# Block-sparse attention, then a gated MLP, on one core: gate and value products taken in turns, and more filler matmuls at the start

## The chip, the core and the metric

The kernel runs on one core of a Trainium2 chip. The metric is the device time of one execution in microseconds (us), the median over several runs. A core has a matrix engine (TensorE, PE in the profile; its weight loads are shown as PEld), VectorE (DVE), ScalarE (ACT), GpSimd (POOL), and SyncE (SP), which here only issues DMAs. Each engine takes its instructions in program order; they wait for one another through semaphores. [...]

## What is computed

The reference, cut to what matters (4 batches, 8 heads, 768 positions, head size 64, so a model width of 512; d_ff is 1024):

```python
scores = scale * np.matmul(q, k.transpose(0, 1, 3, 2))
scores = np.where(mask, scores, -1000000000.0)   # blocks of 32: band, first, last, sampled
attn = softmax(scores)
x = attn @ v                                      # heads side by side: (4, 768, 512)
...
h = np.maximum(x @ w_in, 0.0)
u, v = (h[..., :d_ff // 2].copy(), h[..., d_ff // 2:].copy())
mu = np.mean(v, axis=-1, keepdims=True)
var = np.mean((v - mu) ** 2, axis=-1, keepdims=True)
v_n = (v - mu) / np.sqrt(var + 1e-06)
v_s = np.einsum('ts,bsd->btd', w_spatial, v_n) + b_spatial[None, :, None]
gated = u * v_s
return (gated @ w_out).astype(np.float32)
```

The second part is the gMLP. Half of `x @ w_in` is the gate u, the other half is the value v. Every position's v is normalized over its 512 features; the spatial product then mixes all 768 positions, so it needs all of the normalized v of a batch.

## The kernel before, in words

**Attention.** The 32 heads are worked off one after another, two (a pair) per outer step `p`. A head's 768 keys are cut into six chunks of 128. One chunk of one head is a slot: two score matmuls of 384 columns (L289) into a PSUM tile with two buffers, one exp on ACT that empties it (L293), and, seven slots behind (`LAG`), the six matmuls of attention times values for one chunk of queries (L305). After the last chunk of a head DVE takes the reciprocal of the row sums and scales (L318, L319). The mask enters as 24 extra rows of q and k. The loads, the casts on POOL (L109, L112), the transposes (by PE in the first pairs, by DMA on SP's queue later) and DVE's copies into the head tiles (L244, L278) for the pairs to come are written into fixed slots of a pair.

**gMLP.** `moe_units` makes a list of single matmuls for one batch, in this order: value products (six chunks of 128 positions, four matmuls of 512 columns each), gate products (six of four), spatial products (six of six), output products (six of four): 108 matmuls. `add` (L376) makes the steps of one product: the first asks for a PSUM tile, the last calls the epilogue. The lists of batches 0, 1 and 2 go into a queue (`moe_q`, L524) once a batch's four pairs are through, and the loop hands out 108/48 = 2.25 matmuls per slot (108/52 for batch 2). These products share a PSUM tag, "moe", of two buffers: the third product from now cannot begin before the epilogue of the first has read its tile. Batch 3 is worked off after the attention (L529 to L532), with six buffers taken in rotation from three tags (`moe_ps(last)`).

**Epilogues.** A value product's `v_post` (L392) applies relu on DVE (L396; in the last batch on ACT, L394), then DVE's statistics (L399) and their aggregation into mean and variance (L400); after chunks 2 and 5, POOL adds epsilon (L403) and raises to the power -0.5 (L405), for three chunks at a time, into `rstd`. A gate product's `u_post` (L411) applies relu on ACT (L412), and DVE normalizes the value chunk of the same number (L413) into `vn`, which it can do once `rstd` is there. A spatial product reads the six chunks of `vn` in order, so its sixth matmul waits for the last of them; its epilogue multiplies by the gate (L430, DVE). In the last batch PE transposes the result (L423), in the others SP's queue does by DMA. An output product is copied out by ACT or DVE (L448, L450) and stored.

**Start.** While the first loads come in, PE runs filler matmuls on zeros (`keep_warm`, L178): eight of 512 columns, then small groups of 128 columns between the work that the first scores need. That work is, in PE's order: the transposes of k's first head (`tr_head`, L228, copied out by DVE, L220), two fillers, the mask product (L252, copied out by ACT), the transposes of q's first head (L228, copied by DVE), six fillers, then the first scores.

Of the kernel before, what the change touches and what calls it, by code (L numbers as in the profile page):

```python
# [10 lines left out]
FP32 = mybir.dt.float32  # L11
BF16 = mybir.dt.bfloat16
I32 = mybir.dt.int32
AF = mybir.ActivationFunctionType
ALU = mybir.AluOpType
# [11 lines left out]
def kernel(  # L27
# [16 lines left out]
    nc = tc.nc  # L44
# [5 lines left out]
    NCH = S // 128  # L50
    HALF = S // 2
    DM = H * D
    DFF = moe_w_in.shape[1]
    DH = DFF // 2
    NDM = DM // 128
# [8 lines left out]
    work = ctx.enter_context(tc.tile_pool(name="work", bufs=1))  # L64
# [5 lines left out]
    w_in_t = const.tile([128, NDM, DFF], BF16)  # L70
# [4 lines left out]
    mhalf = const.tile([128, NCH], FP32)  # L75
# [102 lines left out]
    def keep_warm(n, cols):  # L178
        for _ in range(n):
            nc.tensor.matmul(out=wps[:, 0:cols], lhsT=warm[:, 0:128], rhs=warm[:, 0:cols],  # L180
                             start=True, stop=True)
# [26 lines left out]
    for r in range(NR):  # L208
        nc.vector.scalar_tensor_tensor(out=allowed, in0=colidx,
                                       scalar=samp_f[:, 2 * r:2 * r + 1], in1=allowed,  # L210
                                       op0=ALU.is_equal, op1=ALU.max)
    bm = const.tile([NB, NB], BF16)
    nc.vector.tensor_scalar(out=bm, in0=allowed, scalar1=1.0, scalar2=-MASK_NEG,
                            op0=ALU.subtract, op1=ALU.mult)
# [3 lines left out]
                         func=AF.Copy)  # L218
# [3 lines left out]
    def act_copy(o, i):  # L222
        nc.scalar.activation(out=o, in_=i, func=AF.Copy)

    def tr_head(h, nm, copy):
        ps = psum.tile([128, S], BF16, tag="moe", bufs=2)
        for c in range(NCH):
            nc.tensor.transpose(out=ps[0:D, c * 128:(c + 1) * 128], in_=nat[nm, 0][:, c, h],  # L228
                                identity=ident)
        copy((qt if nm == "q" else kt)[h][0:D, :], ps[0:D, :])  # L230
# [15 lines left out]

    tr_head(0, "k", dve_copy)
    nc.vector.tensor_copy(out=kt[0][D:KR, :], in_=ind)
    keep_warm(2, 128)
    mq = psum.tile([128, 1024], FP32, tag="sc", bufs=2, name="mq")  # L250
    for hf in range(2):
        nc.tensor.matmul(out=mq[0:NB, hf * 512:hf * 512 + HALF], lhsT=bm,  # L252
                         rhs=ind[:, hf * HALF:(hf + 1) * HALF], start=True, stop=True)
    act_copy(qt[0][D:KR, :].rearrange("p (b c) -> p b c", b=2),
             mq[0:NB].rearrange("p (b c) -> p b c", b=2)[:, :, 0:HALF])
    tr_head(0, "q", dve_copy)
    keep_warm(6, 128)

    def mask_rows(sl):
        nc.vector.tensor_copy(out=kt[sl][D:KR, :], in_=kt[0][D:KR, :])  # L260
# [92 lines left out]
    def moe_ps(last):  # L353
        if not last:
            return psum.tile([128, 512], FP32, tag="moe", bufs=2, name="ps_moe")
        tail_tags.rotate(-1)
        if tail_tags[0] == "sc":
            return psum.tile([128, 1024], FP32, tag="sc", bufs=2, name="ps_sc")[:, 0:512]
        return psum.tile([128, 512], FP32, tag=tail_tags[0], bufs=2, name="ps_t")

    def moe_units(b):
        last = b == B - 1
        units = []
        un = work.tile([128, NCH, DH], BF16, tag="un", bufs=2)
        vsb = work.tile([128, NCH, DH], BF16, tag="vsb", bufs=2)
        vn = work.tile([128, NCH, DH], BF16, tag="vn", bufs=2)
        gn = work.tile([128, NCH, DH], BF16, tag="gn", bufs=2)
        gt = work.tile([128, NCH, NDH, 128], BF16, tag="gt", bufs=2)
        mv = work.tile([128, NCH, 2], FP32, tag="mv", bufs=2)
        std = work.tile([128, NCH], FP32, tag="std", bufs=2)  # L370
        rstd = work.tile([128, NCH], FP32, tag="rstd", bufs=2)

        def xt(g):
            return xt_ref[b * NG + g]

        def add(n, operands, post):  # L376


            box = []

            def step(i):
                if i == 0:
                    box.append(moe_ps(last))
                lhs, rhs = operands(i)
                nc.tensor.matmul(out=box[0], lhsT=lhs, rhs=rhs,  # L385
                                 start=(i == 0), stop=(i == n - 1))
                if i == n - 1:
                    post(box[0])
            units.extend((lambda i=i: step(i)) for i in range(n))

        for tcc in range(NCH):
            def v_post(ps, tcc=tcc):  # L392
                if last:
                    nc.scalar.activation(out=vsb[:, tcc, :], in_=ps, func=AF.Relu)  # L394
                else:
                    nc.vector.tensor_scalar(out=vsb[:, tcc, :], in0=ps, scalar1=0.0,  # L396
                                            scalar2=None, op0=ALU.max)
                stats = work.tile([128, 6], FP32, tag="stats", bufs=2)
                nc.vector.bn_stats(out=stats, in_=vsb[:, tcc, :])  # L399
                nc.vector.bn_aggr(out=mv[:, tcc, :], in_=stats)  # L400
                if tcc % 3 == 2:
                    cs = slice(tcc - 2, tcc + 1)
                    nc.gpsimd.tensor_scalar(out=std[:, cs], in0=mv[:, cs, 1], scalar1=1e-6,  # L403
                                            scalar2=None, op0=ALU.add)
                    nc.gpsimd.tensor_tensor(out=rstd[:, cs], in0=std[:, cs],  # L405
                                            in1=mhalf[:, cs], op=ALU.pow)
            add(NDM, lambda g, tcc=tcc: (xt(g)[:, tcc * 128:(tcc + 1) * 128],
                                         w_in_t[:, g, DH:DFF]), v_post)

        for tcc in range(NCH):  # L410
            def u_post(ps, tcc=tcc):  # L411
                nc.scalar.activation(out=un[:, tcc, :], in_=ps, func=AF.Relu)  # L412
                nc.vector.tensor_scalar(out=vn[:, tcc, :], in0=vsb[:, tcc, :],  # L413
                                        scalar1=mv[:, tcc, 0:1],
                                        scalar2=rstd[:, tcc:tcc + 1],
                                        op0=ALU.subtract, op1=ALU.mult)
            add(NDM, lambda g, tcc=tcc: (xt(g)[:, tcc * 128:(tcc + 1) * 128],
                                         w_in_t[:, g, 0:DH]), u_post)

        def g_tr(tcc):  # L420
            ps = psum.tile([128, S], BF16, tag="moe", bufs=2, name="ps_g")
            for dhc in range(NDH):
                nc.tensor.transpose(out=ps[:, dhc * 128:(dhc + 1) * 128],  # L423
                                    in_=gn[:, tcc, dhc * 128:(dhc + 1) * 128],
                                    identity=ident)
            act_copy(gt[:, tcc].rearrange("p c n -> p (c n)"), ps[:, 0:DH])

        for tcc in range(NCH):
            def s_post(ps, tcc=tcc):
                nc.vector.scalar_tensor_tensor(out=gn[:, tcc, :], in0=ps,  # L430
                                               scalar=b_col[:, tcc:tcc + 1],
                                               in1=un[:, tcc, :], op0=ALU.add, op1=ALU.mult)
                if not last:
                    nc.sync.dma_start_transpose(out=gt[:, tcc], in_=gn[:, tcc, :])
                elif tcc > 0:
                    g_tr(tcc - 1)
            add(NCH, lambda sc, tcc=tcc: (w_spt[:, sc, tcc * 128:(tcc + 1) * 128],
                                          vn[:, sc, :]), s_post)

        for tcc in range(NCH):  # L440
            def o_post(ps, tcc=tcc):
                osb = work.tile([128, DM], FP32, tag="osb", bufs=6)
                if last and tcc == NCH - 1:
                    nc.scalar.activation(out=osb[:, 0:DM // 2], in_=ps[:, 0:DM // 2],
                                         func=AF.Copy)
                    nc.vector.tensor_copy(out=osb[:, DM // 2:DM], in_=ps[:, DM // 2:DM])
                elif tcc % 2 == 0:
                    nc.scalar.activation(out=osb, in_=ps, func=AF.Copy)  # L448
                else:
                    nc.vector.tensor_copy(out=osb, in_=ps)  # L450
                nc.sync.dma_start(
                    out=out[b].rearrange("(p c) d -> c p d", c=NCH)[tcc], in_=osb)
            if last and tcc == 1:
                units.append(lambda: g_tr(NCH - 1))
            add(NDH, lambda dhc, tcc=tcc: (gt[:, tcc, dhc, :], w_out_t[:, dhc, :]), o_post)
        return units
# [7 lines left out]
    for p in range(NP + 1):  # L464
        for s in range(12):
            g = 12 * p + s
# [54 lines left out]
            if s == 8 and p >= NG:  # L521
                xtr(p - 1)
                if p % NG == 0:
                    moe_q.extend(moe_units(p // NG - 1))  # L524
                    slots_left = 48 if p < NP - NG else 52
                    budget = 0.0
    for _ in range(len(moe_q) // 2):
        moe_q.popleft()()
    xtr(NP - 1)  # L529
    moe_q.extend(moe_units(B - 1))  # L530
    while moe_q:
        moe_q.popleft()()  # L532
# [28 lines left out]
```

The softmax here doesn't subtract the row's maximum and nothing guards it: scores larger than these inputs give would overflow.

## Time and profile before

| | |
|---|---|
| median of 5 runs | 225.96 us (224.1 to 226.25) |
| the profiled execution, device time | 226.05 us |
| its span, first to last instruction | 224.3 us |
| first scores (L289) start | 8.04 us |
| first gMLP product starts | 50.7 us |
| first product of the last batch starts | 195.6 us |
| busy: PE, ACT, DVE, POOL | 216.6, 177.7, 128.7, 64.7 us |

The device time is 1.75 us longer than the span; all positions in the text are us from the span's start. In a line of the timeline or of a group, the tile written stands to the left of the arrow, the tiles read to the right; what stands in brackets is how long the engine sat idle before it and what released it. PE's instructions overlap, so that the duration of one is not its price: in a dense row a matmul of 512 columns starts 0.216 us after the one before it, though each is shown 0.38 long. The same holds for ACT: an exp is shown 0.82 long, and in a dense row six take 4.21 us.

### The profile page before, as it was taken

To read this page: it belongs to the slowest core of one execution; us is meant where nothing else is said; L and a number is where in the kernel's file an instruction comes from. 1 tells how busy PE (TensorE), PEld (TensorE's weight loads), DVE (VectorE), ACT (ScalarE), POOL (GpSimd) and SP (SyncE) were. 2 spreads that over 40 slices of the span, in tenths; PEclk is the share of its full clock that TensorE was granted. 3 is DMA by queue.
4 is the path that set the end of the run, shared out by engine and by line. 5 is a ranking of instruction groups with operands and counts; after the bars stand their busy time and mean duration, and the time that the engine had idled before them with its cause. 6 is when DMAs were issued, how large, how long until landed. Compare 5 with 4: busy or idle time off the path is not lost.

```text
span 224.3 us, 5316 instructions
## 1 busy us (share of the span) xinstructions
PE 216.6 (97%) x2148; PEld 130.6 (58%) x2148; DVE 128.7 (57%) x282; ACT 177.7 (79%) x246; POOL 64.7 (29%) x88
## 2 busy tenths in 40 slices
PE   7999999999999999999899999999999999999993
PEld 3567777775555655665556566566556655544551
DVE  5465554556984545268983454359993433584531
ACT  5599999998789888887699888888899885266351
POOL 5435751429950801210650301210620000012000
PEclk9999999999999999999999999999999999999999
DMA  6689989895799676999756296999050224620015
GB/s 200 222 294 390 382 287 378 286 127 61 219 296 149 229 119 158 232 293 279 238 105 214 47 109 190 223 291 271 3 105 5 57 50 82 212 96 0 0 52 230
DMA packets 56092, 40.25 MB, mean 179 GB/s; under 512 B 39300, under 2 KB 51588, under 8 KB 56068
## 3 DMA queue, kind: packets, MB, share of 16 engines
q1 hardware_dynamic: 55780, 39.53, 66.1%
q10 hardware_dynamic: 288, 0.39, 0.6%
q8 instruction: 16, 0.26, 0.5%
q14 instruction: 8, 0.07, 0.1%
HBM read 24.38 MB, written 6.29 MB: 137 GB/s over the span
## 4 chain that ended last, share of the span: by engine, by line
PE 71%; DVE 14%; ACT 13%; issue 1%
PE ps_moe L385 25%; PE ps L289 19%; ACT a_all L293 12%; PE ps_av L305 10%; PE ps_t L385 7%; DVE vsb L396 4%; DVE stats L399 4%; PE ps_sc L385 3%; PE wps L180 2%; DVE kt L278 2%; DVE xn L319 2%; PE ps L228 1%; DVE mv L400 1%; PE ps_x L329 1%; PE ps_g L423 1%
## 5 line engine op out<-in xcount | busy, mean ns | idle before, releaser
L293 ACT ACTIVATE a_all<-ps 128x768 bf16<-128x768 f32 x192 | 150.0, 816 | 21.7 <-PE ps L289 13.7
L289 PE MATMUL ps<-qt,kt 88*128 88x384 bf16 x384 | 94.5, 327 | 1.3 <-DVE qt L244 0.5
L305 PEld LDWEIGHTS <-a_all 128*128 128x128 bf16 x1152 | 60.4, 97 | 39.3 <-issue 3.4
L305 PE MATMUL ps_av<-vv,a_all 128*128 128x65 bf16 x1152 | 67.8, 194 | 0.0
L385 PE MATMUL ps_moe<-w_in_t,xt 128*128 128x512 bf16 x144 | 43.0, 378 | 1.3 <-DVE vsb L396 0.8
L385 PE MATMUL ps_moe<-vn,w_spt 128*128 128x512 bf16 x108 | 31.8, 378 | 0.0
L289 PEld LDWEIGHTS <-kt 88*128 88x128 bf16 x384 | 28.3, 98 | 4.0 <-issue 1.2
L112 POOL CAST vv<-st_v 128x768 bf16<-128x768 f32 x16 | 13.6, 847 | 55.9 <-PE ps_av L305 52.0
L385 PEld LDWEIGHTS <-xt 128*128 128x128 bf16 x192 | 18.6, 97 | 16.1 <-issue 0.3
L430 DVE SCALAR_TENSOR_TENSOR gn<-ps_moe,b_col,un 128x512 bf16<-128x512 f32 x18 | 13.5, 748 | 18.4 <-PE ps_moe L385 18.3
L318 DVE RECIPROCAL rc<-ps_av 128x6 f32<-128x6 f32 x32 | 6.1, 190 | 25.8 <-PE ps_av L305 25.7
L385 PE MATMUL ps_moe<-w_out_t,gt 128*128 128x512 bf16 x72 | 20.7, 378 | 0.1
L403 POOL TENSOR_SCALAR std<-mv 128x3 f32<-128x3 f32 x8 | 2.0, 246 | 63.2 <-DVE mv L400 63.1
L385 PEld LDWEIGHTS <-w_spt 128*128 128x128 bf16 x144 | 13.7, 97 | 10.8
L319 DVE TENSOR_TENSOR xn<-ps_av,rc 128x384 bf16<-128x384 f32 x32 | 17.8, 557 | 1.1
L109 POOL CAST nat_k<-st_k 128x768 bf16<-128x768 f32 x15 | 12.6, 839 | 17.2 <-DMA st_k<-in_k_dram 8.9
L399 DVE BATCH_NORM_STATS2 stats<-vsb 128x6 f32<-128x512 bf16 x24 | 16.7, 694 | 1.5 <-ACT vsb L394 0.8
L396 DVE TENSOR_SCALAR vsb<-ps_moe 128x512 bf16<-128x512 f32 x18 | 12.3, 681 | 3.0 <-PE ps_moe L385 3.0
L109 POOL CAST nat_q<-st_q 128x768 bf16<-128x768 f32 x15 | 13.1, 870 | 0.0
L385 PEld LDWEIGHTS <-gt 128*128 128x128 bf16 x96 | 8.8, 97 | 7.0 <-issue 0.2
L278 DVE COPY kt<-tt_k 64x768 bf16<-64x768 bf16 x20 | 9.5, 476 | 4.8 <-DMA tt_k<-nat_k 4.6
L412 ACT ACTIVATE un<-ps_moe 128x512 bf16<-128x512 f32 x18 | 10.9, 608 | 0.0
(80 smaller groups left out, 173.2 us busy)
## 6 DMA issues: line engine op xcount, KB each, us to landing
st_v<-in_v_dram SPq DMA_DIRECT2D x16, 384.0 KB, 5.2
out_dram<-osb SPq DMA_DIRECT2D x24, 256.0 KB, 2.4
st_q<-in_q_dram SPq DMA_DIRECT2D x15, 384.0 KB, 4.4
st_k<-in_k_dram SPq DMA_DIRECT2D x15, 384.0 KB, 5.1
wst<-in_moe_w_spatial_dram SPq DMA_DIRECT2D x3, 768.0 KB, 5.9
wst<-in_moe_w_in_dram SPq DMA_DIRECT2D x4, 512.0 KB, 8.6
wst<-in_moe_w_out_dram SPq DMA_DIRECT2D x2, 512.0 KB, 6.6
st_k<-in_k_dram ACTq DMA_DIRECT2D x2, 192.0 KB, 2.9
```

The source lines that it names most:

```text
L109: eng.tensor_copy(out=dst, in_=src)
L112: nc.gpsimd.tensor_copy(out=vv[p % 3][:, :, :, 0:D], in_=st.pop(("v", p)).rearrange("p h (c d) -> p h c d", d=D))
L278: nc.vector.tensor_copy(out=(qt if nm == "q" else kt)[(2 * p + h) % 4][0:D, :], in_=src[h * D:(h + 1) * D, :])
L289: nc.tensor.matmul(out=ps[:, hf * 512:hf * 512 + HALF], lhsT=kt[j % 4][:, ci * 128:(ci + 1) * 128], rhs=qt[j % 4][:, hf * HALF:(hf + 1) * ...
L293: nc.scalar.activation(out=a_ref[j][:, ci, :].rearrange("p (b c) -> p b c", b=2), in_=ps.rearrange("p (b c) -> p b c", b=2)[:, :, 0:HALF], ...
L305: nc.tensor.matmul(out=av_ref[j][:, qc, :], lhsT=a_ref[j][:, ci, qc * 128:(qc + 1) * 128], rhs=vv[p % 3][:, h, ci, :], start=(ci == 0), st ...
L319: nc.vector.tensor_tensor(out=xn_ref[p][:, :, h, :], in0=ps[:, :, 0:D], in1=rc.to_broadcast([128, NCH, D]), op=ALU.mult)
L385: nc.tensor.matmul(out=box[0], lhsT=lhs, rhs=rhs, start=(i == 0), stop=(i == n - 1))
L396: nc.vector.tensor_scalar(out=vsb[:, tcc, :], in0=ps, scalar1=0.0, scalar2=None, op0=ALU.max)
L399: nc.vector.bn_stats(out=stats, in_=vsb[:, tcc, :])
L412: nc.scalar.activation(out=un[:, tcc, :], in_=ps, func=AF.Relu)
L430: nc.vector.scalar_tensor_tensor(out=gn[:, tcc, :], in0=ps, scalar=b_col[:, tcc:tcc + 1], in1=un[:, tcc, :], op0=ALU.add, op1=ALU.mult)
```

## The change

Two things are changed. First, the order of the twelve input products of a batch: instead of six value products and then six gate products, they come as v0, v1, v2, u0, v3, u1, v4, u2, v5, u3, u4, u5. The spatial and output products stay where they were. The epilogue of the gate product `tcc` now normalizes value chunk `tcc - 1`, and the last one normalizes chunks 4 and 5; the pairs of POOL's L403 and L405 stay with value chunks 2 and 5. Second, six filler matmuls of 128 columns are added ahead of the first scores: two more behind the k transposes, two between the mask product and the q transposes, two more behind the q transposes.

```diff
     tr_head(0, "k", dve_copy)
     nc.vector.tensor_copy(out=kt[0][D:KR, :], in_=ind)
-    keep_warm(2, 128)
+    keep_warm(4, 128)
     mq = psum.tile([128, 1024], FP32, tag="sc", bufs=2, name="mq")
...
+    keep_warm(2, 128)
     tr_head(0, "q", dve_copy)
-    keep_warm(6, 128)
+    keep_warm(8, 128)
...
-        for tcc in range(NCH):
-            def v_post(ps, tcc=tcc):
...
-            add(NDM, lambda g, tcc=tcc: (xt(g)[:, tcc * 128:(tcc + 1) * 128],
-                                         w_in_t[:, g, DH:DFF]), v_post)
-
-        for tcc in range(NCH):
-            def u_post(ps, tcc=tcc):
-                nc.scalar.activation(out=un[:, tcc, :], in_=ps, func=AF.Relu)
-                nc.vector.tensor_scalar(out=vn[:, tcc, :], in0=vsb[:, tcc, :],
-                                        scalar1=mv[:, tcc, 0:1],
-                                        scalar2=rstd[:, tcc:tcc + 1],
-                                        op0=ALU.subtract, op1=ALU.mult)
-            add(NDM, lambda g, tcc=tcc: (xt(g)[:, tcc * 128:(tcc + 1) * 128],
-                                         w_in_t[:, g, 0:DH]), u_post)
+        def v_post(tcc, ps):
...
+        def normalize(tcc):
+            nc.vector.tensor_scalar(out=vn[:, tcc, :], in0=vsb[:, tcc, :],
+                                    scalar1=mv[:, tcc, 0:1],
+                                    scalar2=rstd[:, tcc:tcc + 1],
+                                    op0=ALU.subtract, op1=ALU.mult)
+
+        def u_post(tcc, ps):
+            nc.scalar.activation(out=un[:, tcc, :], in_=ps, func=AF.Relu)
+            if tcc > 0:
+                normalize(tcc - 1)
+            if tcc == NCH - 1:
+                normalize(tcc)
+
+        def in_proj(tcc, cols, post):
+            add(NDM, lambda g: (xt(g)[:, tcc * 128:(tcc + 1) * 128], w_in_t[:, g, cols]),
+                lambda ps: post(tcc, ps))
+
+        for i in range(NCH + 2):
+            if i < NCH:
+                in_proj(i, slice(DH, DFF), v_post)
+            if i >= 2:
+                in_proj(i - 2, slice(0, DH), u_post)
```

The body of `v_post` is unchanged.

More of the change, by code (lines that the diff above doesn't have):

```diff
@@ L389, in add @@
             units.extend((lambda i=i: step(i)) for i in range(n))
-        for tcc in range(NCH):
-            def v_post(ps, tcc=tcc):
[L393 to L406, printed above, removed]
-            add(NDM, lambda g, tcc=tcc: (xt(g)[:, tcc * 128:(tcc + 1) * 128],
-                                         w_in_t[:, g, DH:DFF]), v_post)
@@ L410, in moe_units @@
-        for tcc in range(NCH):
-            def u_post(ps, tcc=tcc):
-                nc.scalar.activation(out=un[:, tcc, :], in_=ps, func=AF.Relu)
-                nc.vector.tensor_scalar(out=vn[:, tcc, :], in0=vsb[:, tcc, :],
-                                        scalar1=mv[:, tcc, 0:1],
-                                        scalar2=rstd[:, tcc:tcc + 1],
-                                        op0=ALU.subtract, op1=ALU.mult)
-            add(NDM, lambda g, tcc=tcc: (xt(g)[:, tcc * 128:(tcc + 1) * 128],
-                                         w_in_t[:, g, 0:DH]), u_post)
+        def v_post(tcc, ps):
+            if last:
+                nc.scalar.activation(out=vsb[:, tcc, :], in_=ps, func=AF.Relu)
+            else:
+                nc.vector.tensor_scalar(out=vsb[:, tcc, :], in0=ps, scalar1=0.0,
+                                        scalar2=None, op0=ALU.max)
+            stats = work.tile([128, 6], FP32, tag="stats", bufs=2)
+            nc.vector.bn_stats(out=stats, in_=vsb[:, tcc, :])
+            nc.vector.bn_aggr(out=mv[:, tcc, :], in_=stats)
+            if tcc % 3 == 2:
+                cs = slice(tcc - 2, tcc + 1)
+                nc.gpsimd.tensor_scalar(out=std[:, cs], in0=mv[:, cs, 1], scalar1=1e-6,
+                                        scalar2=None, op0=ALU.add)
+                nc.gpsimd.tensor_tensor(out=rstd[:, cs], in0=std[:, cs],
+                                        in1=mhalf[:, cs], op=ALU.pow)
```

## Prediction

> **What bounds the kernel now.** I read the page's totals first, then the slices and the chain of work that ended last.
>
> ```profile
> PE 216.6 (97%) x2148; PEld 130.6 (58%) x2148; DVE 128.7 (57%) x282; ACT 177.7 (79%) x246; POOL 64.7 (29%) x88
> ...
> DVE  5465554556984545268983454359993433584531
> ACT  5599999998789888887699888888899885266351
> ...
> PE 71%; DVE 14%; ACT 13%; issue 1%
> ```
>
> TensorE is the bound by name. A slice is 5.6 us. Before the tail the DVE row has three places at 8 or 9 (slices from 56, 101 and 151 us on): there the value products of batches 0, 1 and 2 lie. The second view is the table by stretches for batch 1, first its value products, then its gate products.
>
> ```profile
> core 0: us, PE busy (x) PEld busy (x) DVE busy (x) ACT busy (x) POOL busy (x), PEclk, DMA share, GB/s
> ...
> 103.50:114.30 10.80, 10.01 (x103) 5.88 (x101) 10.31 (x22) 8.37 (x11) 3.70 (x5) 1.00 0.74 204
> 114.30:125.00 10.70, 10.70 (x113) 6.38 (x111) 5.47 (x15) 10.44 (x17) 4.72 (x7) 1.00 0.61 163
> ```
>
> In the first stretch DVE is busy 10.31 of 10.80 us and PE only 10.01; in the second DVE has half its time free, ACT 10.44 of 10.70, and PE loses nothing. The third view is the timeline where PE loses most.
>
> ```profile
> 109.91 0.49 PE L289 MATMUL ps<-qt,kt 88*128 88x384 bf16 x2
> ...
> 110.52 0.67 DVE L396 TENSOR_SCALAR vsb<-ps_moe 128x512 bf16<-128x512 f32 x1
> ...
> 111.25 0.38 PE L385 MATMUL ps_moe<-w_in_t,xt 128*128 128x512 bf16 x1 [0.64 <-DVE vsb L396]
> ...
> 111.66 0.49 PE L289 MATMUL ps<-qt,kt 88*128 88x384 bf16 x2
> 112.61 0.49 PE L289 MATMUL ps<-qt,kt 88*128 88x384 bf16 x2
> ```
>
> Each score pair (L289) opens a slot. The slot from 111.66 to 112.61, with two gMLP matmuls, is undisturbed: 0.95 us. The one from 109.91 takes 1.75, because the next product's accumulator is one that DVE has still to empty (two buffers). So many such slots are what the interleaving can give back. From 13 to 49.5 us ACT sets the pace instead (35.71 busy of 36.40, exps 0.70 apart); from 195 us on the last batch runs alone, with PE dense.
>
> **Part 1, interleaving in batches 0 to 2.** No instruction is added or removed; the order of twelve products, and the place of vn (L413), change. I list the slots with two gMLP matmuls that are too long in the value stretches, by the starts of their L289: 60.56 to 61.78, 62.73 to 64.00, 109.91 to 111.66, 112.61 to 113.87, 160.22 to 161.45, 162.41 to 163.67. They sum to 7.99 us, six undisturbed ones to 5.70: 2.29 us lost. Does the new order hold? A product is 4 matmuls at 2.25 per slot, about 1.78 us. Before, each value product asks DVE for 0.681 (L396) + 0.694 (L399) + 0.182 (L400) = 1.56 us, and the attention for some 0.22 (L318, L319: 0.75 in six slots) and 0.26 (the head copies of L278): 2.04 in 1.78, too much. After, a value and a gate product together have 3.57 us, and ask DVE for 1.56 + 0.41 (vn) + 0.97 = 2.94 (82%), ACT for 0.60 (relu) and 3.57 exps of 0.70, 2.5: 3.1 (87%). Both fit. Only the first three value products still stand nearly in a row, and DVE's backlog was then some 0.4 us (second relu of batch 1 at 103.56, the third due at 105.4, begun at 105.79). A gain of 2.2; between 0 and 2.29.
>
> New waits: vn of chunk 0 to 2 now stands in DVE's queue at the sixth to tenth product, where rstd is two to three products (4 us and more) old; that of chunk 3 stands two products after the last value product, some 3.6 us, against 3 us for relu, statistics and POOL's power. If DVE does wait there, L318, L319 and L278 are behind it; they are needed three or more slots later. POOL's own queue: the pair of L403 and L405 for chunks 3 to 5 moves behind the casts of the next pair, and the casts of the pair after it then stand behind L403's wait; these casts are read ten slots later, and SP's transposes of them with them. No DMA is reordered: SP's queue has no instruction in this part. Cost 0.
>
> **Part 2, the same order in the last batch.** Here nothing needs to be relieved (both epilogues use ACT, six buffers), PE runs without a hole, and the last value product is the ninth instead of the sixth. The timeline of its chain:
>
> ```profile
> 201.01 0.60 ACT L394 ACTIVATE vsb<-ps_t 128x512 bf16<-128x512 f32 x1 [0.27 <-PE ps_t L385]
> ...
> 201.64 0.69 DVE L399 BATCH_NORM_STATS2 stats<-vsb 128x6 f32<-128x512 bf16 x1
> ...
> 203.03 0.89 POOL L405 TENSOR_TENSOR rstd<-std,mhalf 128x3 f32<-128x3 f32 x1
> ...
> 203.95 1.06 DVE L413 TENSOR_SCALAR vn<-vsb,mv,rstd 128x512 bf16<-128x512 bf16 x3 [0.45 <-POOL rstd L405]
> ...
> 205.99 1.46 PE L385 MATMUL ps_sc<-vn,w_spt 128*128 128x512 bf16 x6
> ```
>
> From the sixth relu (201.01) to vn of chunk 3 it is 2.94 us, and vn is complete at 205.01, a us before PE wants it. Three products later (the ninth relu stands at 203.60 here) the same chain gives vn 3 from 206.54 to 206.92, then 0.34 each: 207.26 and 207.60. PE starts the first spatial product at 205.99 as before, its fourth matmul would start at 206.64 and waits until about 206.95, the fifth until 207.3, the sixth until 207.64; the second product starts at 207.86 instead of 207.28. **0.58 us lost**, and since PE is dense to the end, it is paid in full. What is late next (gn, its transposes, the outputs) shifts with it. Bounds: 0.3 (a quicker hand-over) to 0.9 (DVE or POOL slower).
>
> **Part 3, six more fillers.** They are matmuls of 128 columns on PE's own queue, ahead of the first scores.
>
> ```profile
> 1.17 3.60 PE L180 MATMUL wps<-warm 128*128 128x512 bf16 x8 [1.17 <-DVE allowed L171]
> ...
> 7.33 0.82 PE L180 MATMUL wps<-warm 128*128 128x128 bf16 x6
> ...
> 8.04 0.82 PE L289 MATMUL ps<-qt,kt 88*128 88x384 bf16 x2
> ...
> 8.90 4.04 ACT L293 ACTIVATE a_all<-ps 128x768 bf16<-128x768 f32 x5 [1.45 <-PE ps L289]
> ...
> 10.61 0.48 PE L289 MATMUL ps<-qt,kt 88*128 88x384 bf16 x2
> ```
>
> The same pair takes 0.82 at 8.04 and 0.48 from 10.61 on, and 512 columns take 0.45 here against 0.216 in the tail: PE runs at half rate until about 10.3 us, although the row of the granted clock shows 9 in every slice (it does not show this start). Six fillers before the first scores take 8.04 - 7.33 = 0.71, so 0.11 to 0.12 each. Four of the new ones stand ahead of the q transposes (two where PE waited 0.1 us), the last two behind them, where the six old ones already last as long as DVE's copy of q (to 7.98): nothing hides them. First scores and first exp: up to 6 x 0.11 = 0.65 later. The first slots are paced by PE and lose a little less in half rate, since fewer of them now lie before 10.3: I take **0.55** at the sixth exp (13.13), from where ACT is saturated to 49.5 and PE after that, so it is carried to the end.
>
> [...] The row speaks for the cost: PE was recorded busy for 1.90 of 1.90 us between 4.7 and 6.6 and for 2.40 of 2.40 between 6.6 and 9, and still slow, so there is hardly a hole that more fillers could close. [...]
>
> **The sum**, against the profiled execution (span 224.3, time 226.05): 226.05 - 2.2 + 0.58 + 0.55 = 224.98. The median of the runs is 0.09 lower: **224.9**, its own range 224.2 to 225.6.
>
> **Rivals.** [...] Range 222.7 to 224.2, chance 0.28.
> (b) *The middle gives nothing*: DVE stops at vn for POOL's rstd, and the relu behind it keeps PE waiting as before. 226.05 + 1.13, less 0.09: 227.1 at most, 226.1 if half is lost. For it: L413 has waited for L405 in one place (0.45). Against: the 4 us above. Chance 0.14.
> (c) *Slower: ACT holds the accumulators.* A gate product's relu stands behind exps, and two buffers give it 1.78 us. With two exps ahead it needs 2 x 0.81 + 0.60 = 2.2: 0.4 of wait for each of 18 gate products, 7.5 in all, 232. From 0.2 each it decides (224.9 + 3.6 = 228.5). Against: in the gate stretches of before one such relu comes every 1.78 us and PE is busy 10.70 of 10.70. Chance 0.08.
>
> The forecast has 0.50. Less than about 1% cannot be told from no change here: that is 223.7 to 228.2. Faster is most of (a)'s lower half, and a tenth of the forecast with fillers that cost nothing: 0.23. Slower is (c) and a corner of (b): 0.09. The range for 8 in 10 takes in most of (a) and half of (b): 222.9 to 226.4.
>
> **What would show it.** Right: the waits of PE on vsb gone and no slot of two matmuls over 1.0 us in the three value stretches; DVE without a 9 in the slices there; in the tail the first spatial product 2.0 instead of 1.46 long, waiting for DVE's vn; the first exp near 9.5, score pairs of 0.8 before it. [...]

## The result, and the profile after

The changed kernel takes 223.9 us (median of 43 runs, 222.72 to 226.02); the kernel before, run beside it, 224.99 us (80 runs). The ratio is 0.9948, 95% interval 0.9935 to 0.9962: about 1.2 us faster, and inside the bound of 1% within which the prediction called it the same. Ratios here and below leave out executions more than 1.5% above the fastest of their kernel, medians do not. The forecast, 224.9 for 225.96, was a ratio of 0.9953. The 225.96 that it started from was the median of five runs only. The profiled one of them, and by their times probably two more, were of a longer kind that is the less common one: more on this below.

The page after, totals, DVE and ACT slices, shares of the chain:

```profile
PE 214.5 (97%) x2154; PEld 130.0 (59%) x2154; DVE 128.0 (58%) x282; ACT 177.2 (80%) x246; POOL 64.1 (29%) x88
...
DVE  5556455457868455358767544378775433666531
ACT  5699999998899888888899878888989884265351
...
PE 81%; ACT 14%; DVE 2%; issue 1%; POOLq 0%; POOL 0%
```

DVE does the same work, but its three full places have sunk to 6 to 8 tenths, and its share of the chain fell from 14% to 2%. The share of busy PE says nothing: 97% before and after. The two stretches of batch 1, at about the places to which they have moved:

```profile
core 0: us, PE busy (x) PEld busy (x) DVE busy (x) ACT busy (x) POOL busy (x), PEclk, DMA share, GB/s
100.80:111.60 10.80, 10.80 (x113) 6.53 (x112) 8.90 (x21) 9.58 (x13) 3.51 (x5) 1.00 0.84 245
111.60:122.30 10.70, 10.70 (x112) 6.37 (x111) 7.42 (x17) 10.03 (x15) 4.61 (x7) 1.00 0.55 151
```

DVE's 10.31 and 5.47 have become 8.90 and 7.42 us, and PE is busy all of both. Here are slot starts of that batch, from PE's timeline:

```profile
107.19 0.49 PE L290 MATMUL ps<-qt,kt 88*128 88x384 bf16 x2
...
108.35 0.49 PE L290 MATMUL ps<-qt,kt 88*128 88x384 bf16 x2
...
109.30 0.49 PE L290 MATMUL ps<-qt,kt 88*128 88x384 bf16 x2
...
110.25 0.49 PE L290 MATMUL ps<-qt,kt 88*128 88x384 bf16 x2
...
111.21 0.49 PE L290 MATMUL ps<-qt,kt 88*128 88x384 bf16 x2
```

They are 1.16 (three gMLP matmuls), 0.95, 0.95 and 0.96 apart. None of the six long slots is left in any batch. In the last batch, the chain of the last value product and what PE does meanwhile:

```profile
200.35 0.60 ACT L394 ACTIVATE vsb<-ps_t 128x512 bf16<-128x512 f32 x1 [0.27 <-PE ps_t L386]
...
202.37 0.88 POOL L405 TENSOR_TENSOR rstd<-std,mhalf 128x3 f32<-128x3 f32 x1
202.74 0.81 PE L386 MATMUL ps_sc<-vn,w_spt 128*128 128x512 bf16 x3
203.28 1.06 DVE L409 TENSOR_SCALAR vn<-vsb,mv,rstd 128x512 bf16<-128x512 bf16 x3 [1.10 <-POOL rstd L405]
203.75 1.02 PE L386 MATMUL ps_sc<-vn,w_spt 128*128 128x512 bf16 x3 [0.20 <-DVE vn L409]
204.61 1.46 PE L386 MATMUL ps_t<-vn,w_spt 128*128 128x512 bf16 x6
```

The first spatial product starts at 202.74; without a wait the next would start six matmuls later, at 202.74 + 1.29 = 204.03. It starts at 204.61: 0.58 lost. The bracket shows only 0.20, because PE's matmuls are shown 0.38 long and overlap; the loss is read from the starts. And the start of the kernel:

```profile
7.61 0.50 PE L290 MATMUL ps<-qt,kt 88*128 88x384 bf16 x2
...
8.15 2.92 ACT L294 ACTIVATE a_all<-ps 128x768 bf16<-128x768 f32 x4 [1.01 <-PE ps L290]
...
12.22 2.22 ACT L294 ACTIVATE a_all<-ps 128x768 bf16<-128x768 f32 x3 [0.19 <-PE ps L290]
```

Here the first score pair takes 0.50, not 0.82, and the first exp is 0.75 sooner than in the profile before. The span fell from 224.3 to 221.6 us, 2.6, more than twice what the runs show. It adds up: the sixth exp moved from 13.13 to 12.22 (-0.91); from there to the first spatial product of the last batch it was 192.86 us (to 205.99) and is 190.52 (to 202.74), which gives -2.34 for the middle; the tail took +0.58. Together that is -2.67. The first of these is not the change's doing, as the experiments show.

### The profile page after: what moved, and what is told of

Same layout as the page of the kernel before. It is cut to its first block, busy times and chain, and to the rows that moved or that the text cites. A ratio compares the mean times of both kernels' runs of the same rounds, so it can differ in the third digit from the quotient of the medians.

```text
span 221.6 us, 5325 instructions
## 1 busy us (share of the span) xinstructions
PE 214.5 (97%) x2154; PEld 130.0 (59%) x2154; DVE 128.0 (58%) x282; ACT 177.2 (80%) x246; POOL 64.1 (29%) x88
## 4 chain that ended last, share of the span: by engine, by line
PE 81%; ACT 14%; DVE 2%; issue 1%; POOLq 0%; POOL 0%
PE ps_moe L386 31%; PE ps L290 23%; ACT a_all L294 13%; PE ps_av L306 13%; PE ps_t L386 6%; PE ps_sc L386 3%; PE wps L180 2%; PE ps L228 1%; PE ps_x L330 1%; PE ps_g L434 1%; POOLq L567 0%; DVE gn L441 0%; DVE stats L399 0%; PE ps_tr L239 0%; ACT vsb L394 0%
## 5 line engine op out<-in xcount | busy, mean ns | idle before, releaser
L386 PE MATMUL ps_moe<-w_in_t,xt 128*128 128x512 bf16 x144 | 42.0, 378 | 0.0
L403 POOL TENSOR_SCALAR std<-mv 128x3 f32<-128x3 f32 x8 | 2.2, 278 | 72.1 <-DVE mv L400 59.4
L109 POOL CAST nat_q<-st_q 128x768 bf16<-128x768 f32 x15 | 12.6, 837 | 0.0
L279 DVE COPY kt<-tt_k 64x768 bf16<-64x768 bf16 x20 | 8.5, 427 | 6.1 <-DMA tt_k<-nat_k 5.9
L409 DVE TENSOR_SCALAR vn<-vsb,mv,rstd 128x512 bf16<-128x512 bf16 x24 | 10.3, 448 | 2.6 <-POOL rstd L405 2.6
```

The source lines that it names most:

```text
L109: eng.tensor_copy(out=dst, in_=src)
L279: nc.vector.tensor_copy(out=(qt if nm == "q" else kt)[(2 * p + h) % 4][0:D, :], in_=src[h * D:(h + 1) * D, :])
L386: nc.tensor.matmul(out=box[0], lhsT=lhs, rhs=rhs, start=(i == 0), stop=(i == n - 1))
```

## The experiments

My theory was the prediction's sum: the new order frees the middle of DVE's overload, costs 0.58 in the tail, and the fillers cost a little. The rivals: the gain comes from the fillers, through the clock; or the order gives nothing; or the alternation of the releasing engines matters, not DVE's load. "Ratio" is that to the kernel before on the same chip, with its 95% interval; 0.001 is 0.22 us.

**Six fillers alone**, in the kernel before.

```diff
-    keep_warm(2, 128)
+    keep_warm(4, 128)
...
+    keep_warm(2, 128)
     tr_head(0, "q", dve_copy)
-    keep_warm(6, 128)
+    keep_warm(8, 128)
```

> The kernel before with the six added fillers and nothing else. If fillers only lengthen PE's way to the first scores, as the prediction took it: 0.3 to 0.55 us slower than before, ratio 1.001 to 1.0025, and at an equal onset of the full clock a first exp 0.4 to 0.65 later. [...]

Ratio 1.0012 (0.9991 to 1.0033): no gain can be seen. By luck its profile, like that of before, is of an execution in which PE gets its full clock late (the trace's clock record begins at 10.17 us; before, at 10.28), so the two can be laid side by side:

```profile
8.69 0.85 PE L290 MATMUL ps<-qt,kt 88*128 88x384 bf16 x2
...
9.54 0.80 PE L290 MATMUL ps<-qt,kt 88*128 88x384 bf16 x2
9.58 3.03 ACT L294 ACTIVATE a_all<-ps 128x768 bf16<-128x768 f32 x4 [1.91 <-PE ps L290]
...
13.76 0.81 ACT L294 ACTIVATE a_all<-ps 128x768 bf16<-128x768 f32 x1 [0.18 <-PE ps L290]
```

The first exp is at 9.58 instead of 8.90, the sixth at 13.76 instead of 13.13: 0.68 and 0.63 later. (Only the first part of this profile is used: at 148 us it has a wait for a load of q that no other has.)

**New order alone, in all batches** (the change with the fillers of before).

> The new order in all four batches, with the fillers of before. By the prediction's terms -2.2 in the middle and +0.58 in the tail: 1.6 us faster, ratio 0.993. If the gain of the whole change came from the fillers and the clock: ratio 1.000, and slots of two gMLP matmuls over 1.0 us still there.

Ratio 0.9946 (0.9924 to 0.9968), the whole change's 0.9948. The order alone accounts for the whole gain, within these intervals. The long slots are gone and the tail's wait is there (the second spatial product at 204.75, after a first from 202.89: again 0.57). With the fillers of before, its first exp is at 8.03, also well ahead of 8.90; so the early start of the profile after is no mark of the added fillers.

**New order in batches 0 to 2 alone.**

```diff
-        for i in range(NCH + 2):
+        if not last:
+            for i in range(NCH + 2):
...
+        else:
+            for i in range(NCH):
+                in_proj(i, slice(DH, DFF), v_post)
+            for i in range(NCH):
+                in_proj(i, slice(0, DH), u_post)
```

(in the last batch, gate chunk `tcc` normalizes value chunk `tcc` again; the fillers are those of before).

> The new order in batches 0 to 2 alone; the last batch and the fillers as before. By the prediction's terms 2.2 us faster, ratio 0.990, and the first spatial product of the last batch dense at 1.46 us for six matmuls. If the tail's term is wrong and the late value product costs nothing: the same time as with the new order in all batches.

Ratio 0.9894 (0.9861 to 0.9927), 2.4 us faster, the best version of the study. In the tail the spatial products are dense again, the first two 1.29 apart:

```profile
202.74 1.46 PE L385 MATMUL ps_sc<-vn,w_spt 128*128 128x512 bf16 x6
204.03 1.46 PE L385 MATMUL ps_t<-vn,w_spt 128*128 128x512 bf16 x5
```

**New order in the last batch alone** (the condition turned round; the fillers of before).

> The new order in the last batch alone; batches 0 to 2 and the fillers as before. By the prediction's terms 0.58 us slower, ratio 1.0026, with the wait of the first spatial product on vn. If the wait is made up for later in the tail: ratio 1.000.

Ratio 1.0036 (1.0015 to 1.0058): 0.8 us slower, with 0.58 inside the interval. The trace has the first spatial product at 204.26 and the second at 206.12, 0.57 late.

**New order in the last batch alone, with values one ahead of the gates**, for the dose: the last value product is the tenth.

```diff
-            for i in range(NCH + 2):
+            for i in range(NCH + 1):
...
-                if i >= 2:
-                    in_proj(i - 2, slice(0, DH), u_post)
+                if i >= 1:
+                    in_proj(i - 1, slice(0, DH), u_post)
```

> The order changed in the last batch alone, with the values one ahead of the gates: the last value product is the tenth. If PE waits for the chain from that product's relu to vn, the wait grows by one product, 0.865 us, from 0.58 to 1.44: ratio 1.006 to 1.007. If the wait of 0.58 came from something else (DVE's queue, the order of the vn): unchanged at 0.6.

Ratio 1.0066 (1.0043 to 1.009). The tail's first two spatial products:

```profile
204.49 0.81 PE L385 MATMUL ps_sc<-vn,w_spt 128*128 128x512 bf16 x3
...
206.29 1.02 PE L385 MATMUL ps_sc<-vn,w_spt 128*128 128x512 bf16 x3 [0.99 <-DVE vn L408]
207.15 1.46 PE L385 MATMUL ps_t<-vn,w_spt 128*128 128x512 bf16 x6
```

The second is 207.15 - 204.49 - 1.29 = 1.37 late, 0.79 more than with two ahead, for a product of 0.865. The wait is that chain's.

**Old order, relu of odd value chunks on ACT**, in batches 0 to 2.

```diff
-                if last:
+                if last or tcc % 2:
                     nc.scalar.activation(out=vsb[:, tcc, :], in_=ps, func=AF.Relu)
```

> The order of before; in batches 0 to 2 the relu of the odd value chunks is done by ACT instead of DVE. If the middle gained because DVE's load per value product (2.04 us in 1.78) was the bound: 1.7 in 1.78 now, so most of the 2.2 us comes back without any new order, ratio 0.990 to 0.993, and no long slots. If the order itself mattered, because ACT and DVE must alternate as releasers: ratio 0.997 or more.

Ratio 0.9931 (0.991 to 0.9953). Without any new order most of the gain is there; PE is busy 10.80 of 10.80 in the value stretch of batch 1, DVE 9.06 and ACT 10.10. Five of the six long slots are gone. One is left, in batch 2, where PE still waits for DVE's relu, and it loses 0.51 us (158.50 - 157.04 - 0.95):

```profile
157.04 0.49 PE L289 MATMUL ps<-qt,kt 88*128 88x384 bf16 x2
...
158.09 0.38 PE L385 MATMUL ps_moe<-w_in_t,xt 128*128 128x512 bf16 x1 [0.35 <-DVE vsb L396]
...
158.50 0.49 PE L289 MATMUL ps<-qt,kt 88*128 88x384 bf16 x2
```

From the sixth exp to the first spatial product of the last batch, a stretch that leaves out the start and the tail, the traces have 192.86 us before, 191.13 here, 190.53 with the new order in the middle, and 192.78 with the new order in the last batch alone. So taking work off DVE in the value stretches gives 1.7 of the 2.3 us, and the new order is only one way to do it. This run alone does not refute the rival of the alternation, for here too DVE and ACT release the products in turns; the next run bears on that.

**Values three ahead of the gates, in all batches** (`NCH + 3`, `i - 3`; fillers of before).

> Value products three ahead of the gates instead of two, in all batches, with the fillers of before. The last value product of the last batch is then the eighth: its chain ends 0.86 us sooner, so the wait of 0.58 in the tail is gone. In the middle a fourth value product stands in a row, which may leave a wait of 0.3 per batch. Ratio 0.990 if the middle stays free of waits, 0.994 if each batch waits again.

Ratio 0.9913 (0.9881 to 0.9944). No long slot of the six is left in the middle, and there is no wait in the tail (spatial products at 203.66 and 204.96, 1.30 apart). The added value product in a row does no harm, though DVE alone releases four products one after another: a strict alternation is not what PE needs. And the chain has the 0.86 that it needs. It is the middle-only version in one order for all batches; the two intervals overlap.

**Middle order with the six fillers.**

> The new order in batches 0 to 2 alone, as in the run with the new order in the middle (ratio 0.989), with the six fillers of the change added. If the fillers cost time: 0.3 us more than without them, ratio 0.991. If they bring the clock sooner: ratio 0.987 to 0.989.

Ratio 0.9935 (0.9905 to 0.9964), against 0.9894 (0.9861 to 0.9927) without. The medians are 222.97 and 222.8. The sign is that of a cost, but the intervals overlap: not decided by time.

**No small fillers ahead of the first scores**, first in the kernel before, then with the middle order; and **twenty more** instead of six (8, 6 and 14 added in the three places).

> The kernel before without the eight small fillers ahead of the first scores (the eight of 512 columns at the very start stay). If small fillers only lengthen PE's way: the same or a little faster, 0 to 0.4 us, since the last six lie beside DVE's copy and only two are in the way. [...]

> The new order in batches 0 to 2 alone, and none of the eight small fillers ahead of the first scores. If they only take time: 2.2 us of the order and up to 0.2 more, ratio 0.989. If they matter for the clock, as the run without them (ratio 1.002) may say: ratio 0.991 to 0.993.

> The kernel before with twenty fillers added ahead of the first scores instead of the change's six (eight, six and fourteen in the three places). If fillers only take time, at 0.056 (full clock) to 0.11 us each, less what lies beside DVE's copy: 0.8 to 2 us slower, ratio 1.004 to 1.009, with the full clock no sooner. If they bring the full clock sooner, the late first exps go away and the cost is made up in part: ratio below 1.003.

Ratios: without, 1.002 (0.9992 to 1.0047) and, with the middle order, 0.9902 (0.9874 to 0.9929); twenty more, 1.0023 (1.0001 to 1.0045). Neither fewer nor more is faster. Without them and with the middle order, the median of all 22 executions, 223.28 against 225.02, is a ratio of 0.9923: six long ones are not in the 0.9902. The traces give the price at a known onset of the full clock (the start of the clock record that is stored with each trace), in us:

| fillers ahead of the first scores | full clock from, and first exp (one execution each) |
|---|---|
| none | 4.45: 7.27; 5.89: 7.79 |
| eight, as before | 4.46: 7.40; 4.81: 7.52; 5.00: 7.62; 6.04: 8.03; 6.25: 8.13; 10.28: 8.90; 10.42: 8.90 |
| fourteen, as after | 5.49: 8.15; 6.56: 8.61; 10.17: 9.58 |
| twenty-eight | 5.40: 8.66 |

At an onset of 5.4 to 5.5, the row of eight gives about 7.8: six more cost 0.35, twenty 0.9, none at all saves 0.2. At an onset near 10.2 six cost 0.68. At every onset that can be compared, fillers cost.

Where the 0.35 lies shows when the profile after (onset 5.49) is laid beside that of the run with values one ahead (eight fillers, onset 5.00). The two behind the k transposes add 0.10 (they and the first two last 0.32, not 0.22, to the mask product). The two ahead of the q transposes put the transposes 0.64 us behind the start of the mask product, not 0.42: 0.22. The last two add 0.01, since with eight the first scores wait for DVE's copy of q anyway:

```profile
7.08 0.50 PE L289 MATMUL ps<-qt,kt 88*128 88x384 bf16 x2 [0.20 <-DVE qt L220]
```

Yet the times say less than these prices: 0.9 us for twenty fillers became 0.5 us, and leaving all small ones out gained nothing. The spread of the spans tells more. Of 133 executions of the kernel before, 92 have spans of 222.2 to 223.65 and 40 of 224.0 and more, with one between. With the change's six fillers alone, 6 of 22 have 224.8 or more, so the late group is still there. With twenty more, all 15 lie between 223.3 and 224.7, with no gap. Without the small fillers, 9 of 22 have 224.9 or more.

The upper group is likely that of the executions with a late onset. The three profiles with an onset after 10.1 us all have long spans for their kernel (224.3, 226.3, 223.2), and none of the other ten has; and a late onset moves the sixth exp from between 11.48 and 12.21 to 13.13, about the distance of the two groups. It is not shown, since only profiled executions have a clock record.

The other executions have a mean granted clock, and it shows a second effect. The mean counts from the first record on: in the profile before, with its onset at 10.28, it is 1.000, so a late onset does not lower it. It is 0.998 or more in 132 of the 133 executions before. In four of the nine long ones without the small fillers it is 0.982 to 0.985, and in five of the 22 with the middle order 0.985 to 0.988. By that mean these nine ran some 5 to 8 us at half rate after the full clock had come (an estimate, with the 0.5 that the records before and after show behind the end of the full clock: twice the missing share of about 215 us; of this at most 1.2 us lies at the very end in the profiles). So the eight small fillers of before do more than take time. None of these executions was profiled, and where the clock fell is not known.

## Why the prediction was right

**The middle, -2.2.** Right in place, mechanism and size. The six slots that the prediction listed, 2.29 us, are all gone after, and the order in the middle alone gains 2.4 us (interval 1.6 to 3.1). That it is DVE's load is shown by the run that moves half of the relus to ACT, together with the one in which DVE releases four products in a row and PE does not wait. The new waits were as harmless as argued: DVE's vn now waits 2.6 us for POOL's rstd in four places, 1.1 of it in the tail, and the trace puts no wait of PE down to the rest. Rival (b), that these waits eat the gain, and rival (c), that ACT holds the accumulators, are refuted: PE waits for neither vsb nor un in the middle.

**The tail, +0.58.** Right to the hundredth in the trace, with the working that was given: from the relu to vn 2.93 us (203.28 - 200.35; 2.94 assumed). It is paid to the end of the kernel: the run with the tail alone costs 0.3 to 1.3 us, and one product more of delay costs another 0.79 in the trace.

**The fillers, +0.55.** Right in sign, too large for most executions. The 0.55 holds for the profiled execution, with its full clock from 10.3 us (0.63 was measured there, at the sixth exp). At the earlier onset that most executions seem to have, six fillers cost 0.35, and the prediction's "nothing hides them" is wrong there for the last two, which lie beside DVE's copy of q. By time the six cost 0.3 (interval -0.2 to 0.7).

**Rival (a), the earlier clock.** A first exp before 8.9 with pairs of about 0.5 is in the profile after, but it is no mark of the added fillers: the fillers of before show it as well, in five of the profiles above. Over the thirteen profiles the full clock begins at 4.45 to 6.56 us in ten and at 10.17 to 10.42 in three, one of these with the six fillers and two without. The record lasts 215.04 us in eight, 218.45 in four and 211.63 in one, in steps of 3.41 us. So a single profile cannot compare two kernels in the first 10 us. The three late onsets lie 9 us and more behind the first matmul (1.17). In the profile before PE was recorded busy for 9.11 of the 9.11 us in between; what delays the full clock there stays open.

No run shows the size of the gain on which this rival's range, 222.7 to 224.2, and its chance of 0.28 rest. What the runs show in its place is a first exp anywhere from 7.40 to 8.90 with the same eight fillers, and a ratio of 1.0012 (0.9991 to 1.0033) for six more.

The prediction took the cost because PE's busy rows left hardly a hole for more fillers to close. The sign came out right, but that reason was not enough. A larger dose of fillers does seem to take away the late executions (none of 15 in the upper group, where 30% would be 4 or 5), and without the small ones there are more long ones (9 of 22), in part by a clock that fell back. Six show neither.

**The base.** The prediction took 225.96 as the kernel's time; over 80 runs it is 224.99. The sum's differences were right, and the absolute time 223.9 is a us under the forecast's 224.9 for this reason, not for one of its terms. That it lies in rival (a)'s range is chance.

What stays open: whether the upper group of spans is the late onset (likely, above); where the clock fell in the executions without the small fillers; and whether six fillers are worth their price in the best version (0.9894 without, 0.9935 with, overlapping).

## What to carry to other kernels

When two kinds of products with epilogues on different engines come in blocks, price each block apart: an engine that was busy for 57% of the kernel had 115% of the time's work in a block (2.04 us per 1.78 us). Mixing the blocks gave all of the loss back, moving part of the epilogue most of it. The same reordering costs where a later step needs all of one kind, so choose the order by stage: here the middle alone gains 2.4 us, twice the whole change, and values three ahead give nearly the same with one order. Before a difference in the first microseconds is put down to a change, compare profiles of the same onset of the full clock, or time many executions.

## What was not expected of the hardware

The slow start shows only in the durations (0.82 us against 0.50 for the first score pair, before and after) and in the start of the clock record (10.28 and 5.49 us), not in the row of the granted clock, which has a 9 in each of the 40 slices of both. And it is not fixed by the work: the instructions ahead of the first scores are the same in seven profiles, and the full clock came at 4.46 to 6.25 us in five of them and at 10.28 and 10.42 in two. That costs up to 1.5 us at the first exp (7.40 against 8.90). What sets the onset no run here shows.
